# Layer-norm transposes moved from TensorE to DMA in a two-layer attention and SwiGLU kernel

## The chip, the cores and the metric

One core of a Trainium2 chip. The metric is device time in microseconds (us) of one execution; lower is better. Medians of four to seven executions are quoted. Engine names in the profile: PE is TensorE (matrix multiply), PEld its weight loads, DVE is VectorE, ACT is ScalarE, POOL is GpSimd, SP is SyncE, which issues DMAs here. A DMA "lands" when its data has arrived; "landing" times count from its issue. "SPq" and "ACTq" are the instruction queues of SP and ACT.

## The reference

Two layers, each an attention block A and a gated feed-forward block B, on 2048 tokens of width 1024, with a layer norm before each block. Both layers use the same weights.

```python
def _layernorm(x, axis=-1, eps=1e-5):
    m = jnp.mean(x, axis=axis, keepdims=True); v = jnp.var(x, axis=axis, keepdims=True)
    return (x - m) / jnp.sqrt(v + eps)
# A: q, k, v = x @ wqkv, 32 heads of 32; each token attends to 8 tokens, 2 apart, looking back; then @ wo
# B: (silu(x @ w1) * (x @ w3)) @ w2, inner width 3584
x = A_x
x = x + _A_ref(_layernorm(x), A_wqkv, A_wo)
x = x + _B_ref(_layernorm(x), B_w1, B_w3, B_w2)
x = x + _A_ref(_layernorm(x), A_wqkv, A_wo)
x = x + _B_ref(_layernorm(x), B_w1, B_w3, B_w2)
```

## The kernel before

The tokens are cut into four chunks of 512. A "Q" stage computes q, k and v of a chunk on PE and stores them to DRAM; a "T" stage loads them and does the windowed attention on DVE, with a projection by wo on PE; a "B" stage is the feed-forward of a chunk. Stages of different chunks are interleaved so that PE has matmuls while DVE does attention. A scheduler orders each engine's instructions when the program is built, from estimated times and priorities; at run time each engine works through its own list in that order.

This kernel's matmuls take both operands with the contraction dimension on the 128 partitions, so every normalized chunk `xn` (tokens on partitions) must be transposed into `xnT` (features on partitions). Before, PE does it into PSUM and ACT copies it out:

```python
def ln_chunk(c, psum):
    with hp():                                   # raises the priority by 3000 instructions
        xnT = xtp.tile([P, KT, CH], BF16, name="xnT")          # 2 buffers
        ...                                      # bn_stats, bn_aggr on DVE, sqrt on ACT
        for j in range(TPC):                     # 4 tiles of 128 tokens
            n = c * TPC + j
            xn = xnp.tile([P, D], BF16, name="xn")             # 2 buffers
            nc.vector.tensor_scalar(xn[:], x_sb[:, n, :], mv[:, j, 0:1], rstd[:, j:j + 1],
                                    op0=ALU.subtract, op1=ALU.mult)
            pT = psum.tile([P, KT, P], BF16, name="pT", tag="mm")
            for kk in range(KT):                 # 8 blocks of 128x128
                nc.tensor.transpose(pT[:, kk, :], xn[:, kk * P:(kk + 1) * P], ident[:])
            nc.scalar.copy(xnT[:, :, j * P:(j + 1) * P], pT[:])
    return xnT
```

The first chunk has its own function, which the change leaves on PE. The Q stage, cut, with the DMAs:

```python
for which in range(3):                           # q, k, v
    w = wA.tile([P, KT, D], BF16, name="wqkv", tag="wA")       # 2 MB, 2 buffers, loaded for every chunk
    ... nc.sync.dma_start(w[:, k0:k1, :], wqkv_v[...])
    for t0 in range(0, KT, SG):
        sgt = stg.tile([P, SG, CH], BF16, name="sgt")          # 3 buffers
        ... # 16 matmuls into ps, copied to sgt by ACT
        nc.sync.dma_start(qkv_d[l][which][:, t0:t0 + SG, c * CH:(c + 1) * CH], sgt[:])
    if which == 1 and ln_next is not None:
        pending_ln[ln_next] = ln_chunk(ln_next[1], psQ)        # next chunk's norm
```

All DMAs (weights, stores, loads of q, k, v) are issued from SyncE's one in-order queue.

## Time and profile before

| | before |
|---|---|
| median time | 1692.33 us (1691.25 to 1693.8) |
| PE busy | 1661.5 of 1695.0 us |
| PE transposes after the first chunk | 480, 35.0 us busy, 12.7 us idle just before them |
| DVE, ACT busy | 1142.3, 378.7 us |
| DMA queue | 288 MB, 52.7% of 16 engines |

The profile of before is of an execution of 1696.81 us, not one of the four in the table and slower than all of them; its granted clock was 0.995. From its page, the table of engines (busy us, share of the span, number of instructions):

```profile
PE 1661.5 (98%) x7952; PEld 823.1 (49%) x7952; DVE 1142.3 (67%) x1930; ACT 378.7 (22%) x561; POOL 1.9 (0%) x12
q1 hardware_dynamic: 282800, 288.25, 52.7%
```

PE is the bound: 98% busy. The second line is the DMA queue: packets, MB, and the time of its packets as a share of 16 engines' span.

Groups of instructions by line and shape, before: count, then busy us and mean ns of one, then the idle time of the engine just before them with what ended it.

```profile
L132 PE MATMUL pT<-ident,xn 128*128 128x128 bf16 x480 | 35.0, 224 | 12.7 <-DVE xn L128 9.6 <-DVE x_sb L313 1.4 <-ACT sgt L199 0.6
L133 ACT COPY xnT<-pT 128x1024 bf16<-128x1024 bf16 x60 | 57.7, 1024 | 158.1 <-PE pT L132 153.3 <-PE ps L197 4.7
```

This is the work that the change takes off PE and ACT. The 12.7 us are PE standing still in front of a transpose, mostly for DVE's xn.

### The profile page before, as it was taken

To read this page: it belongs to the slowest core of one execution; us is meant where nothing else is said; L and a number is where in the kernel's file an instruction comes from. 1 tells how busy PE (TensorE), PEld (TensorE's weight loads), DVE (VectorE), ACT (ScalarE), POOL (GpSimd) and SP (SyncE) were. 2 spreads that over 40 slices of the span, in tenths; PEclk is the share of its full clock that TensorE was granted. 3 is DMA by queue.
4 is the path that set the end of the run, shared out by engine and by line. 5 is a ranking of instruction groups with operands and counts; after the bars stand their busy time and mean duration, and the time that the engine had idled before them with its cause. 6 is when DMAs were issued, how large, how long until landed. Compare 5 with 4: busy or idle time off the path is not lost.

```text
span 1695.0 us, 19762 instructions
## 1 busy us (share of the span) xinstructions
PE 1661.5 (98%) x7952; PEld 823.1 (49%) x7952; DVE 1142.3 (67%) x1930; ACT 378.7 (22%) x561; POOL 1.9 (0%) x12
## 2 busy tenths in 40 slices
PE   8999999999999999999999999999999999999999
PEld 5655644444444444554445544455444554444444
DVE  5699999999996821229982399813997159952112
ACT  3433422212213101132022321223212221121100
POOL 0000000000000000000000000000000000000000
PEclk9999999999999999999999999999999999999999
DMA  9976655554454244475434754356542654435443
GB/s 315 325 242 201 223 167 160 174 164 149 142 170 148 95 160 146 149 241 182 128 122 155 244 179 148 97 195 229 185 145 95 200 161 151 149 108 191 149 149 99
DMA packets 282891, 289.51 MB, mean 171 GB/s; under 512 B 6192, under 2 KB 256048, under 8 KB 282672
## 3 DMA queue, kind: packets, MB, share of 16 engines
q1 hardware_dynamic: 282800, 288.25, 52.7%
q8 instruction: 62, 1.02, 0.2%
q14 instruction: 29, 0.24, 0.0%
HBM read 258.87 MB, written 29.36 MB: 170 GB/s over the span
## 4 chain that ended last, share of the span: by engine, by line
PE 51%; DVE 39%; DMA 4%; issue 4%; ACT 2%; DVEq 0%; SPq 0%; ACTq 0%
PE acc L308 15%; PE pu L290 11%; PE pg L286 11%; PE ps L197 10%; DVE tm L261 6%; DVE pr L220 5%; DVE hT L295 4%; PE po L268 3%; DVE pr L170 3%; DVE tm L170 3%; DVE st L119 2%; DVE pr L171 2%; DVE tm L171 2%; DMA qkv_d_1_170<-sgt 2%; DVE x_sb L313 1%
## 5 line engine op out<-in xcount | busy, mean ns | idle before, releaser
L290 PE MATMUL pu<-xnT,w3t 128*128 128x512 bf16 x1792 | 430.9, 380 | 0.0
L286 PE MATMUL pg<-xnT,w1t 128*128 128x512 bf16 x1792 | 430.8, 380 | 0.1
L308 PE MATMUL acc<-w2t,hT 128*128 128x512 bf16 x1792 | 392.7, 379 | 0.8 <-DVE hT L295 0.8
L197 PE MATMUL ps<-xnT,wqkv 128*128 128x512 bf16 x1536 | 340.8, 382 | 4.8 <-ACT sgt L199 3.2
L294 ACT ACTIVATE sg<-pg 128x512 bf16<-128x512 f32 x224 | 133.7, 597 | 679.5 <-PE pg L286 662.9
L197 PEld LDWEIGHTS <-wqkv 128*128 128x128 bf16 x1536 | 220.2, 144 | 118.3 <-issue 10.3
L286 PEld LDWEIGHTS <-w1t 128*128 128x128 bf16 x1792 | 175.5, 98 | 209.0 <-issue 2.2
L290 PEld LDWEIGHTS <-w3t 128*128 128x128 bf16 x1792 | 175.5, 98 | 208.4 <-issue 1.6
L308 PEld LDWEIGHTS <-hT 128*128 128x128 bf16 x1792 | 174.9, 98 | 209.5 <-DVE hT L295 1.5
L220 DVE TENSOR_TENSOR pr<-qT,kT 128x2048 bf16<-128x2048 bf16 x128 | 153.6, 1213 | 170.1 <-DMA kT<-qkv_d_1_170 158.2
L295 DVE TENSOR_TENSOR hT<-sg,pu 128x512 bf16<-128x512 bf16 x224 | 152.0, 679 | 170.8 <-PE pu L290 162.7
L313 DVE TENSOR_TENSOR x_sb<-x_sb,acc 128x512 bf16<-128x512 bf16 x128 | 87.0, 681 | 147.6 <-PE acc L308 147.6
L199 ACT CAST sgt<-ps 128x512 bf16<-128x512 f32 x192 | 112.0, 586 | 229.4 <-PE ps L197 200.9
L261 DVE TENSOR_TENSOR tm<-At,vT 128x2048 bf16<-128x2048 bf16 x128 | 152.8, 1215 | 0.1
L268 PE MATMUL po<-wo,oT 128*128 128x512 bf16 x512 | 127.6, 381 | 7.8 <-DVE oT L172 6.5
L133 ACT COPY xnT<-pT 128x1024 bf16<-128x1024 bf16 x60 | 57.7, 1024 | 158.1 <-PE pT L132 153.3
L268 PEld LDWEIGHTS <-oT 128*128 128x128 bf16 x512 | 48.9, 97 | 89.8 <-DVE oT L172 39.5
L170 DVE TENSOR_TENSOR pr<-pr 128x1024 bf16<-128x1024 bf16 x128 | 86.0, 678 | 0.0
L170 DVE TENSOR_TENSOR tm<-tm 128x1024 bf16<-128x1024 bf16 x128 | 84.6, 682 | 0.0
L119 DVE BATCH_NORM_STATS2 st<-x_sb 128x6 f32<-128x512 bf16 x120 | 75.7, 672 | 6.8 <-DMA x_sb<-in_A_x_dram 6.5
L272 DVE TENSOR_TENSOR x_sb<-x_sb,po 128x1024 bf16<-128x1024 bf16 x32 | 38.7, 1210 | 25.1 <-PE po L268 25.1
L171 DVE TENSOR_TENSOR pr<-pr 128x512 bf16<-128x512 bf16 x128 | 52.2, 414 | 0.1
(203 smaller groups left out, 514.5 us busy)
## 6 DMA issues: line engine op xcount, KB each, us to landing
w1t<-in_B_w_dram SPq DMA_DIRECT2D x56, 1024.0 KB, 5.3
w3t<-in_B_w_dram SPq DMA_DIRECT2D x56, 1024.0 KB, 7.2
w2t<-in_B_w_dram SPq DMA_DIRECT2D x48, 1024.0 KB, 5.4
wqkv<-in_A_wqkv_dram SPq DMA_DIRECT2D x23, 2048.0 KB, 8.1
w2t<-in_B_w_dram SPq DMA_DIRECT2D x16, 512.0 KB, 5.1
qkv_d_0_166<-sgt SPq DMA_DIRECT2D x16, 256.0 KB, 4.8
qkv_d_1_167<-sgt SPq DMA_DIRECT2D x16, 256.0 KB, 5.0
qT<-qkv_d_0_166 SPq DMA_DIRECT2D x8, 512.0 KB, 4.8
```

The costliest lines, as they stand in the source:

```text
L170: nc.vector.tensor_tensor(buf[:, 0:4, :], buf[:, 0:4, :], buf[:, 4:8, :], op=ALU.add)
L171: nc.vector.tensor_tensor(buf[:, 0:2, :], buf[:, 0:2, :], buf[:, 2:4, :], op=ALU.add)
L197: nc.tensor.matmul(ps[:], lhsT=w[:, kk, t::KT], rhs=xnT[:, kk, :], start=(kk == 0), stop=(kk == KT - 1))
L199: nc.scalar.copy(sgt[:, t - t0, :], ps[:])
L220: nc.vector.tensor_tensor(pr[:], qT[:], kT[:, :, k0:k0 + TCH], op=ALU.mult)
L261: nc.vector.tensor_tensor(tm[:], At[:], win, op=ALU.mult)
L268: nc.tensor.matmul(ps[:, hh, :], lhsT=oT[:, t, j * P:(j + 1) * P], rhs=wo[:, t, hh * 512:(hh + 1) * 512], start=(t == 0), stop=(t == KT - 1))
L286: nc.tensor.matmul(pg[:], lhsT=w1t[:, kk, fi * P:(fi + 1) * P], rhs=xnT[:, kk, :], start=(kk == 0), stop=(kk == KT - 1))
L290: nc.tensor.matmul(pu[:], lhsT=w3t[:, kk, fi * P:(fi + 1) * P], rhs=xnT[:, kk, :], start=(kk == 0), stop=(kk == KT - 1))
L294: nc.scalar.activation(sg[:], pg[:], ACTF.Silu)
L295: nc.vector.tensor_tensor(hT[:, g0 + fi - f0, :], sg[:], pu[:], op=ALU.mult)
L308: nc.tensor.matmul(acc[:], lhsT=hT[:, f - f0, j * P:(j + 1) * P], rhs=w2ts[(f - f0) // 8][:, (f - f0) % 8, :], start=(f == f0), stop=(f == ...
```

## The change

Intent: PE is the bound, so take the transposes off it, and let the DMA hardware transpose from SBUF to SBUF. The norm of the next chunk is also emitted earlier, to give the slower path more lead. A tile that only warmed PE up was dropped, and some small buffers were cut, to make room for a third xn.

```diff
-    xnp = ctx.enter_context(tc.tile_pool(name="xn", bufs=2))
+    xnp = ctx.enter_context(tc.tile_pool(name="xn", bufs=3))
...  (the warm-up matmuls read a part of hT in place of a tile of their own; mv1, sd1: 4 -> 2 buffers)
-    def ln_chunk(c, psum):
+    def ln_chunk(c):
...
-                pT = psum.tile([P, KT, P], BF16, name="pT", tag="mm")
-                for kk in range(KT):
-                    nc.tensor.transpose(pT[:, kk, :], xn[:, kk * P:(kk + 1) * P], ident[:])
-                nc.scalar.copy(xnT[:, :, j * P:(j + 1) * P], pT[:])
+                nc.sync.dma_start_transpose(out=xnT[:, :, j * P:(j + 1) * P], in_=xn[:])
...
-            if which == 1 and ln_next is not None:
-                pending_ln[ln_next] = ln_chunk(ln_next[1], psQ)
+            if which == 0 and ln_next is not None:
+                pending_ln[ln_next] = ln_chunk(ln_next[1])
```

More of the change, by code (lines that the diff above doesn't have):

```diff
@@ L96 @@
         nc.sync.dma_start(x_sb[:, j:j + 1, :], xin[:, j:j + 1, :])
-    warm = const.tile([P, CH], BF16, name="warm")
-    nc.vector.memset(warm[:], 0.0)
-    preload = small.tile([P, 1], FP32, name="preload")
+    hT = const.tile([P, HTN, CH], BF16, name="hT")
+    nc.vector.memset(hT[:, 0, :], 0.0)
+    preload = small.tile([P, 1], FP32, name="preload", bufs=1)
     nc.scalar.activation(preload[:], epst[:], ACTF.Sqrt)
@@ L102 @@
         pw = psB.tile([P, CH], FP32, name="pw", tag="mm")
-        nc.tensor.matmul(pw[:], lhsT=warm[:, 0:P], rhs=warm[:], start=True, stop=True)
-    hT = const.tile([P, HTN, CH], BF16, name="hT")
+        nc.tensor.matmul(pw[:], lhsT=hT[:, 0, 0:P], rhs=hT[:, 0, :], start=True, stop=True)
     wo = const.tile([P, KT, D], BF16, name="wo")
@@ L141, in stats @@
             st = small.tile([P, 2, 6], FP32, name="st1")
-            mv = small.tile([P, 2], FP32, name="mv1", bufs=4)
+            mv = small.tile([P, 2], FP32, name="mv1", bufs=2)
             for hh in range(2):
@@ L145, in stats @@
             nc.vector.bn_aggr(mv[:], st[:])
-            sd = small.tile([P, 1], FP32, name="sd1", bufs=4)
+            sd = small.tile([P, 1], FP32, name="sd1", bufs=2)
             nc.scalar.activation(sd[:], mv[:, 1:2], ACTF.Sqrt, bias=epst[:])
@@ L178, in q_stage @@
         if xnT is None:
-            xnT = ln_first() if (l, c) == (0, 0) else ln_chunk(c, psQ)
+            xnT = ln_first() if (l, c) == (0, 0) else ln_chunk(c)
         for which in range(3):
@@ L274, in b_stage @@
     def b_stage(c, last):
-        xnT = ln_chunk(c, psB)
+        xnT = ln_chunk(c)
         for (f0, f1) in fsplits:
```

## The prediction

> **What bounds the kernel now.** TensorE. The page's first table has PE busy 1661.5 of 1695.0 us (98%); DVE 1142.3 (67%), ACT 378.7 (22%), DMA 52.7% in the queue table. The chain of waits is 51% PE. The 7424 large matmuls issue every 216 ns in long runs (128 acc matmuls in 27.63 us), an estimate of 1603 us together. So about 90 us of the span is not large matmuls, and only that can be won. In stretches of 50 us DVE is also full from 100 to 500 us (48 to 50 us), and DMA only from 0 to 100 us (0.91 and 0.99).
>
> **What is removed.** 480 PE transposes with their 60 PSUM copies. Groups by line: 35.0 us PE busy, 12.7 us PE idle just before them (9.6 of it waiting for xn on DVE), 57.7 us ACT (60 x 1024 ns). In the timeline a group of eight displaces about 0.45 to 0.6 us of PE or more. Together about 48 us of PE time, almost all on PE's path, since PE is hardly idle elsewhere (33.5 us in total). The norm of a gate/up stage now takes its PSUM slots from the pool of the accumulators, in program order, so its transposes sit at the stage's boundary (540 to 547 us). Without PSUM they can run a stage ahead.
>
> **What is added.** 60 DMA transposes of 256 KB, SBUF to SBUF, 15.7 MB beside 289.5 MB: bandwidth is no problem on average. The Trainium skill, "DMA: Bandwidth & Descriptors", section "Latency and other measured facts", gives 261 GB/s for one kernel's transposes; an estimate from that is 1.0 us each, 60 us of full DMA. No run here shows it yet. I expect 3 to 8 us to landing, since ordinary 256 KB stores here land in 3.2 to 5.0 us. SyncE's queue is in order, and it waits long for buffers to come free (386 us before w2 loads for PE): a transpose can sit behind a waiting load, and a later load behind a transpose that waits for xn. A fourth xn (three buffers) then blocks DVE. Where the norm is computed a stage ahead this is hidden. It is not hidden between 0 and 150 us, where DMA is full, stores of q, k, v are already on the chain (10.9 us at 61 us), and the norm must be ready in a few tens of us; hence the earlier emission between q and k. I charge 5 to 12 us for this.
>
> **Sum.** 1693 - 48 + about 12 = 1657 us. Range 1640 to 1695. Chances: faster by over 2% 0.54, within 2% 0.34, slower 0.12.
>
> **What would show it.** PE busy near 1625 us; no pT group on PE or ACT; ACT near 320 us; PE idle before wqkv and pg matmuls not above a few us per stage, released by the transposes' landing if at all; transposes landing in 3 to 8 us; the start of the first pg right behind the last acc. Matmul spacing stays 216 ns and the granted clock 0.99 or more.
>
> **What would make it wrong.** Transposes of 10 us or more, or slow to issue on SyncE: then weight loads come late, with PE idle before pg, pu and acc, and the time could pass 1700. DVE (full from 100 to 500 us) could swallow the gain there as longer waits for oT. Stores and q/k/v loads held up behind transposes would lengthen the attention stages' wait for kT (158 us now). If none of these bite, the full 48 us give 1645.

## More of the kernel before

Who PE waited for in all of before (us in total, times, longest):

```profile
PE pT L132 <- DVE xn L128: 9.6, 9, 2.7
PE po L268 <- DVE oT L172: 6.5, 13, 2.2
PE ps L197 <- ACT sgt L199: 3.2, 3, 2.0
```

Three stretches of before: PE, PEld, DVE, ACT, POOL busy (instructions), granted clock, DMA share, GB/s. DMA is busiest while the four chunks' q, k, v are computed:

```profile
0.00:160.00 160.00, 146.95 (x727) 92.08 (x728) 124.26 (x228) 60.57 (x96) 1.89 (x12) 0.97 0.83 278
160.00:700.00 540.00, 535.05 (x2557) 252.88 (x2556) 427.54 (x723) 110.97 (x159) 0.00 (x0) 1.00 0.49 156
700.00:1700.00 1000.00, 979.46 (x4672) 478.10 (x4669) 590.49 (x980) 207.11 (x306) 0.00 (x0) 1.00 0.50 161
```

The chain that ended last has two lines that serve as milestones: the first long q/k/v run of layer 1, and the last run of feed-forward accumulations (start, duration):

```profile
708.68 13.83 PE ps L197 x64
...
1670.51 20.73 PE acc L308 x96
```

## The result, and the profile after

The change takes the median from 1692.33 to 1670.78 us (1669.33 to 1672.0). The ratio is 0.9872, with a 95% interval of 0.9855 to 0.9889: 1.3% faster.

The engines and the DMA queue, after:

```profile
PE 1628.0 (98%) x7472; PEld 794.8 (48%) x7472; DVE 1143.0 (69%) x1930; ACT 329.3 (20%) x507; POOL 1.9 (0%) x12
q1 hardware_dynamic: 346160, 303.99, 59.4%
```

The profiled execution is the fastest of the four (1669.33 us, clock 0.997), so the two profiles lie 27 us apart, 6 us more than the medians. PE lost 33.5 us of busy time and ACT 49.4. The span fell by 27.7 us only (1695.0 to 1667.3), so PE's idle time grew from 33.5 to 39.3 us. Where it now stands still (waits of PE, after):

```profile
PE po L264 <- DVE oT L168: 13.6, 15, 2.4
PE ps L193 <- DMA wqkv<-in_A_wqkv_dram: 4.9, 1, 4.9
PE ps L193 <- ACT sgt L195: 4.2, 6, 2.0
PE pT L153 <- DVE xn L150: 3.5, 4, 1.2
```

The 9.6 us in front of transposes are gone, but the waits for DVE's oT have doubled, a wait of 4.9 us for weights appears in a Q stage, and the one for ACT's copies (which wait for stores to free sgt) goes from 3.2 to 4.2 us. The same three stretches, after:

```profile
0.00:160.00 160.00, 143.03 (x645) 88.10 (x646) 125.14 (x229) 49.35 (x85) 1.89 (x12) 0.97 0.96 300
160.00:700.00 540.00, 532.06 (x2448) 246.98 (x2447) 431.06 (x730) 97.92 (x144) 0.00 (x0) 1.00 0.56 167
700.00:1700.00 1000.00, 952.92 (x4383) 459.70 (x4381) 586.78 (x973) 182.06 (x278) 0.00 (x0) 1.00 0.54 167
```

In the first 160 us DMA went from 0.83 to 0.96 busy. The milestones, after:

```profile
699.73 13.83 PE ps L193 x64
...
1643.25 20.73 PE acc L304 x96
```

The kernel is 9.0 us ahead at the first milestone and 27.3 us at the second. Layer 1 alone gained 18.3 us with the transposes of 8 chunks between the milestones, 0.57 us for each group of eight transposes, which is about a group's busy time before (35.0 us / 60 = 0.58). Other runs repeat it: from the first q/k/v matmul of layer 1 to the last accumulation, before took 982.7 us and e8 and e10, which are before in layer 1, 981.5 and 981.1; the change took 964.4, and e3, e9 and e11, which are the change there, 964.0, 965.2 and 963.7. The 7 chunks before the first milestone should have given 16 us at that rate, and gave 9.

Where PE stands still for DVE is much the same in layer 1 with and without the transposes. From 700 us on, the waits for xn and oT together were 9.7 us in before (5.0 and 4.7), and the waits for oT alone were 8.9 us after, 8.7 in e2 and 11.0 in e1 (both below).

What the added DMA looks like, in the answer about the tile xnT, after (duration of the issue in ns, min/median/max, then first and last start in us; the second line is the time from issue to landing):

```profile
L129 SPq DMA_TRANSPOSE xnT<-xn x60: 1231/1302/3577, 23.5 to 1484.5; - x60
...
DMA to landing us min/median/max: 3.1/3.4/8.4
```

PE never waited for a transpose's landing. The last chunk's was issued by 1484.5 us, and its B stage starts at about 1519 (the accumulations before it run from 1498.21 us, for 20.72): there the transposes do run well ahead, as hoped, where before they stood at the stage's boundary.

### The profile page after: what moved, and what is told of

Read it like the earlier page. It is cut to its first block, busy times and chain, and to the rows that moved or that the text cites. A ratio compares the mean times of both kernels' runs of the same rounds, so it can differ in the third digit from the quotient of the medians.

```text
span 1667.3 us, 18841 instructions
## 1 busy us (share of the span) xinstructions
PE 1628.0 (98%) x7472; PEld 794.8 (48%) x7472; DVE 1143.0 (69%) x1930; ACT 329.3 (20%) x507; POOL 1.9 (0%) x12
## 2 busy tenths in 40 slices
DMA packets 346247, 305.18 MB, mean 183 GB/s; under 512 B 69552, under 2 KB 319408, under 8 KB 346032
## 3 DMA queue, kind: packets, MB, share of 16 engines
q1 hardware_dynamic: 346160, 303.99, 59.4%
## 4 chain that ended last, share of the span: by engine, by line
PE 51%; DVE 40%; DMA 4%; issue 4%; ACT 1%; SPq 0%; DVEq 0%; ACTq 0%
PE acc L304 15%; PE pg L282 12%; PE pu L286 12%; PE ps L193 9%; DVE tm L257 6%; DVE pr L216 6%; DVE hT L291 4%; PE po L264 4%; DVE tm L166 4%; DVE pr L166 3%; DVE st L118 2%; DVE tm L167 2%; DVE pr L167 2%; DVE x_sb L309 1%; DVE At L251 1%
## 5 line engine op out<-in xcount | busy, mean ns | idle before, releaser
L264 PE MATMUL po<-wo,oT 128*128 128x512 bf16 x512 | 127.4, 380 | 16.9 <-DVE oT L168 13.6
L167 DVE TENSOR_TENSOR tm<-tm 128x512 bf16<-128x512 bf16 x128 | 51.3, 421 | 0.1
```

What stands on the lines that cost most here:

```text
L167: nc.vector.tensor_tensor(buf[:, 0:2, :], buf[:, 0:2, :], buf[:, 2:4, :], op=ALU.add)
L264: nc.tensor.matmul(ps[:, hh, :], lhsT=oT[:, t, j * P:(j + 1) * P], rhs=wo[:, t, hh * 512:(hh + 1) * 512], start=(t == 0), stop=(t == KT - 1))
```

## The experiments

Two shortfalls needed a cause: the removal was to give 48 us of PE time, and the addition was to cost some 12. Theories, as named in the expectations: **A**, the DMA engines are full at the start and the transposes push weights and stores back; **B**, DVE is full from 100 to 550 us and PE's saved time comes back as waits for DVE; **C**, transposes hold SyncE's in-order queue, and the loads and stores behind them come late. The gain is the median of before minus the median of the run, both from the same rounds.

| run | edit | time, us | gain, us |
|---|---|---|---|
| the change | | 1670.78 | 21.6 |
| e1 | no transposes at all | 1662.57 | 32.0 |
| e2 | PE transposes, rest of the change | 1692.77 | 0.6 |
| e3 | the change, norm emitted between k and v | 1668.29 | 25.1 |
| e4 | layer 0's q/k/v chunks on PE | 1673.45 | 21.1 |
| e5 | every DMA transpose twice | 1725.07 | -31.7 |
| e7 | plain DMA copies in their place | 1679.22 | 14.2 |
| e8, e9 | before, after with less DVE work | 1694.19, 1669.35 | 0.4, 25.2 |
| e10, e11 | before, after with less early DMA | 1692.52, 1665.62 | 1.0, 27.9 |
| e12 | two loads held back | 1675.40 | 18.1 |
| e13 | q/k/v stores from ACT's queue | 1684.84 | 8.0 |

### e1: what the removal is worth when the addition costs nothing

```diff
-                nc.vector.tensor_scalar(xn[:], x_sb[:, n, :], ...)
-                nc.sync.dma_start_transpose(out=xnT[:, :, j * P:(j + 1) * P], in_=xn[:])
+                nc.vector.tensor_scalar(xnT[:, :, j * P:(j + 1) * P], x_sb[:, n, :] (viewed as 128 x 8 x 128), ...)
```

> Wrong result on purpose: DVE writes the normalized rows straight into xnT, so nothing is transposed on any engine (after's order of emission kept). This is the change with its added cost set to zero. After ran at 1670.8 us, 20 us short of the 48 us that the transposes had cost. Theory A (the DMA engines are full for the first 150 us, and the transposes of the first chunks push weight loads and stores back) and theory C (a transpose holds SyncE's in-order queue 1.3 us, and the loads behind it come late) both expect 1655 to 1661 us, with the gain made before 150 us and PE idle before ps down from 10.3 to under 5 us. Theory B (DVE is full from 100 to 550 us, so PE time saved there comes back as waits for oT and hT) expects 1666 to 1671 us, with PE still idle 12 us or more before po.

Measured: 1662.57 us (wrong result, as meant), a gain of 32.0. So the removal is worth 32 us, not 48, and the DMA transposes cost the other 6 to 10 (8.2 by the two medians, 10.4 by the two gains; 5.7 and 6.9 against e3, which will turn out to be the same program as the change). Both A and C and B miss a part: the time is just above A's and C's range, below B's; PE's idle time before ps was 8.3 us, where A and C expected under 5; and the waits for oT that B named are still there. PE and its longest waits in e1:

```profile
PE 1626.8 (98%) x7472; PEld 795.0 (48%) x7472; DVE 1140.8 (69%) x1930; ACT 324.8 (20%) x503; POOL 1.9 (0%) x12
```

```profile
PE po L264 <- DVE oT L168: 15.1, 15, 3.1
PE ps L193 <- ACT sgt L195: 4.6, 4, 2.4
...
PE ps L193 <- DMA wqkv<-in_A_wqkv_dram: 2.6, 1, 2.6
```

The span of e1 was 1661.1 us, so PE was idle 34.3 us: no less than before (33.5). Even with free transposes, the idle time in front of them was not won. PE meets DVE later, at the next instruction that needs it.

```profile
688.59 13.83 PE ps L193 x64
...
1636.89 20.73 PE acc L304 x96
```

Against the change, e1 is 11.1 us ahead at the first milestone and 6.4 at the second. What the DMA transposes cost, they cost early: by 200 us e1 had issued 872 matmuls and the change's run 830, an estimate of 9 us at the 0.216 us of a long run's matmul (64 in 13.83; some records can be missing). Some of this may be start-up luck: from 10 to 20 us the granted clock was 1.00 in e1 and 0.66 in the change's run, and at 20 us e1 was 13 matmuls ahead. But e3, with 0.83 there, was 6 ahead of the change at 20 us and 4 behind at 200, so such a lead need not last. Of the 5 us that e1 loses again later, the clock explains some 3 (an estimate): it was 0.97 from 950 to 1000 and from 1150 to 1200 us in e1, and 1.00 there in the change's run.

### e2: everything but the DMA transposes

```diff
-                nc.sync.dma_start_transpose(out=xnT[:, :, j * P:(j + 1) * P], in_=xn[:])
+                pT = psum.tile(...); 8 x nc.tensor.transpose(...); nc.scalar.copy(xnT[...], pT[:])
```

> Only the emission between q and k and the buffer counts of after; all transposes on PE and ACT as before. If the DMA transposes carry the gain, as theories A and C both say, this is within 5 us of before (1688 to 1698 us). If the earlier emission carries a part, it is below 1685.

Measured: 1692.77 us against 1693.39, nothing: within the range for a gain that the DMA transposes carry. The waits are the point:

```profile
PE po L267 <- DVE oT L171: 11.6, 11, 2.1
...
PE pT L131 <- ACT xnT L132: 2.7, 7, 0.6
...
PE pT L131 <- DVE xn L127: 0.5, 1, 0.5
```

With a third xn and another emission place, the wait in front of the transposes for xn fell from 9.6 to 0.5 us, with the transposes still on PE. The wait for oT rose from 6.5 to 11.6 us, PE's idle time stayed (33.5 and 32.7 us), and so did the median time. So the 12.7 us idle before the transposes were not a separate cost that can be added to their busy time. (The profiled execution was the fastest of e2's four, at 1688.18 us, with a granted clock of 1.000 where the profile of before had 0.995; the 8 us between these two lie in PE's busy time.)

### e3: only the DMA transposes, emission as before

```diff
-            if which == 0 and ln_next is not None:
+            if which == 1 and ln_next is not None:
```

> After, with the next chunk's norm emitted between k and v again. If the placement matters, because DMA transposes need the longer lead, this loses 3 to 10 us against after (1674 to 1681) in the first 150 us, with PE waiting for the transposes' landing before ps. If the scheduler's priority boost places the norm anyway, it stays within 3 us of after's 1671.

Measured: 1668.29 us, 25.1 less than before. A comparison of the built programs shows the same instructions in the same order as the change on PE, DVE, ACT and SP. With DMA transposes the scheduler places the norm alike, wherever it is emitted, as the second case of the expectation has it; this half of the change does nothing. (With PE transposes it does change the order: e2 was built both ways, and the two programs differ.) It is also a repeat of the change: 21.6 and 25.1 us show how far two measurements of one program lie apart, and differences of 3 us below are to be read with that.

### e4: the first layer's q/k/v chunks back on PE

```diff
-                nc.sync.dma_start_transpose(...)                       # all chunks
+                if psum is None: nc.sync.dma_start_transpose(...)      # as before when called for q/k/v chunks 1 to 3
+                else: (8 PE transposes and the copy by ACT)
```

> After, but the norms of q/k/v chunks 1 to 3 of layer 0 are transposed by PE and ACT as before; everything else stays on DMA. In cumulated matmuls after stood 1.8 us behind before at matmul 512 (about 136 us). Theories A and C expect 2 to 6 us gained (1665 to 1669 us), made in the first 150 us, as the DMA engines there are relieved of 12 transposes while PE pays 12 groups of about 0.5 us. Theory B alone expects no gain or a loss of up to 6 us (1670 to 1677).

Measured: 1673.45 us, a gain of 21.1 on before: no better than the change, within B's stated range, outside A's and C's. Within the scatter, 12 DMA transposes cost as much in this stretch as 12 groups on PE do, so placing them by hand on PE wins nothing.

### e8 and e9: room on DVE

```diff
-        for w_ in range(W):
+        for w_ in range(4 if l == 0 else W):      # the other four score products are copied
```

> Wrong result on purpose: before, with half of the DVE score products of layer 0 dropped (4 of 8 shifts, the other 4 copied), some 10 us of DVE work less in each of 8 attention stages between 60 and 550 us. It is the reference for the next run. All theories: between 1670 and 1692 us; DVE no longer full between 100 and 500 us (under 45 of 50 us).

> Wrong result on purpose: after, with the same DVE work dropped. Theory B expects the change to be worth more once DVE has room: 28 to 40 us less than the relieved before, where after is 21.5 us less than before. Theories A and C expect 18 to 24 us, since DMA is as full at the start as it was.

Measured: 1694.19 and 1669.35 us (wrong results, as meant), a difference of 24.8 us, between what the unrelieved program showed twice (21.6 and 25.1). Some 66 us of DVE work (DVE busy 1142.3 to 1076.0 us in before) moved neither kernel. Theory B falls for the stretch that it named: DVE being full in layer 0 is not what eats the gain. All theories missed e8's range, by 2 us. In e9 PE's waits for wqkv were 11.8 us where the change has 4.9: with DVE relieved, PE waited for weights. The test reaches layer 0 only; 8.9 of the change's 13.6 us of waits for oT lie after 700 us, where no DVE work was taken away.

### e5 and e7: more of the transpose, and a plain copy in its place

```diff
+                nc.sync.dma_start_transpose(out=xnT[:, :, j * P:(j + 1) * P], in_=xn[:])   # e5: a second time
...
-                nc.sync.dma_start_transpose(out=xnT[:, :, j * P:(j + 1) * P], in_=xn[:])
+                nc.sync.dma_start(xnT[:, :, j * P:(j + 1) * P], xn[:] (viewed as 128 x 8 x 128))   # e7
```

> After, with every DMA transpose issued twice into the same place (120 in place of 60), same result. Removing them altogether gained 8 us. If their cost is only the full DMA of the first 150 us (theory A) or SyncE's time there (theory C), doubling costs 6 to 14 us, made before 200 us (1677 to 1685 us), and nothing after 700 us, where the norm is a stage ahead. If they cost something in every stage, it is over 15 us, and grows by more than 1 us a stage after 700 us.

> Wrong result on purpose: a plain DMA copy of the same 256 KB from xn to xnT in the transpose's place, the same waits and the same bytes. If bytes on the DMA engines are the cost (theory A as bandwidth) it stays at 1668 to 1672 us. If [...]SyncE's 1.3 us per issue is the cost (theory C), it falls to 1661 to 1666 us, near the run with no transposes (1662.6).

e5 measured 1725.07 us, some 55 us over the change, far above the 6 to 14 that A and C expected. It fits the third case in that text, a cost in every stage: of the loss, 39 us were there at the first milestone (738.37 us) and 56 at the second. But the edit does more than double the cost. The second transpose writes where the first does, so SyncE also waits for the first to land before it issues the second (21.6 us in 14 waits). The waits of PE in e5 show whom that hurts:

```profile
PE ps L194 <- DMA wqkv<-in_A_wqkv_dram: 23.7, 2, 18.9
PE acc L305 <- DMA w2t<-in_B_w_dram: 15.4, 6, 3.8
PE ps L194 <- ACT sgt L196: 14.1, 5, 7.0
PE pu L287 <- DMA w3t<-in_B_w_dram: 8.5, 3, 3.4
```

None of these is a wait for xnT. They are loads and stores that share the queue and the DMA engines with it, in all stages now.

e7 measured 1679.22 us (wrong result, as meant), 8 to 11 us slower than the transposing program, where theory C expected it faster and A the same. Over the whole run the copies' issue was shorter (median 628 ns against 1302), their landing a little later (4.0 us against 3.4). But not where it counts. From 50 to 100 us, first the change, then e7:

```profile
L129 SPq DMA_TRANSPOSE xnT<-xn x4: 1243/1316/3199, 58.1 to 65.6; - x4
DMA to landing us min/median/max: 3.1/4.2/5.7
...
L129 SPq DMA_DIRECT2D xnT<-xn x4: 594/1509/3152, 58.1 to 68.1; - x4
DMA to landing us min/median/max: 2.9/7.2/8.3
```

There a copy was issued no faster than a transpose and landed later, so e7 does not test whether SyncE's issue time is the cost. The loss was made early again, in waits for wqkv (10.4 us) and sgt (9.9 us), in a differently ordered queue; once PE waited 3.4 us for a copy's own landing. The run gives a comparison of cost, too: from the shares of the DMA queue, an estimate of the added DMA time (other transfers' slowing included) is (0.594 x 1667.3 - 0.527 x 1695.0) / 60 = 1.6 us of all 16 engines for a transpose, and (0.578 x 1677.7 - 893.3) / 60 = 1.3 us for the plain copy.

### e10 and e11: room on DMA

```diff
+                if l == 0 and c > 0: k1 = KT // 2            # load half of each q/k/v weight tile, use it twice
                 nc.sync.dma_start(w[:, k0:k1, :], wqkv_v[:, k0:k1, which * D:(which + 1) * D])
```

> Wrong result on purpose: before, loading only the first half of each q/k/v weight tile in chunks 1 to 3 of layer 0 (1 MB in place of 2 MB, nine times) and using it twice. 9 MB less DMA between 45 and 200 us, the same work on every engine. The reference for the next run. Theory A: a small gain on before, 0 to 8 us (1685 to 1693), since its DMA was full only to 100 us.

> Wrong result on purpose: after, with the same 9 MB taken away. Theory A (transposes hurt because the DMA engines are full at the start) expects the difference to the relieved before to grow from 22 to 28-34 us, near what no transposes at all gave (32), with PE waiting for wqkv's landing 2 us or less. Theory C (SyncE's in-order queue is held by the transposes themselves) expects the difference to stay at 20 to 24 us.

Measured: 1692.52 and 1665.62 us (wrong results, as meant). With 9 MB less to load, before gained 1.0 us and the change's kernel 5.2 by its first measurement, 2.7 by e3's. The difference between the two is 26.9 us, between the ranges of A (28 to 34) and C (20 to 24). PE's waits for sgt fell from 4.2 to 1.5 us, but the 4.9 us wait for wqkv stayed, at 4.3. So full DMA engines may be a part of the cost; the evidence, 2 to 5 us, is hardly beyond the scatter of 3.

### e12 and e13: two attempts to do better

```diff
 # e12: a one-column copy by GpSimd makes the load of wo wait for the third score product,
 #      and the first four gate/up weight loads for the k stage of chunk 2 to begin
+                nc.gpsimd.tensor_copy(wo[:, 0, 0:1], psm[:, 2, 0:1])
+                nc.sync.dma_start(wo[:], wo_v)
 # e13
-                nc.sync.dma_start(qkv_d[l][which][...], sgt[:])
+                nc.scalar.dma_start(qkv_d[l][which][...], sgt[:])
```

> After, correct, with 6 MB of loads that are not needed yet taken out of the full stretch: wo waits for the first score products (some 70 us in place of 42 us), the first four gate/up weight tiles wait for the q stage of chunk 2 to end (some 110 us in place of 90 us). Theory A expects 2 to 7 us gained (1664 to 1669 us) before 150 us. Theory C expects no gain (1669 to 1673).

(That text names the q stage of chunk 2; the edit waits for the first k tile after it.)

> After, correct, with the 192 KB-pair stores of q, k and v issued from ACT's queue, right after the copies that fill them; transposes and loads stay on SyncE. The same bytes and the same DMA engines. Theory C (loads and transposes stand in one in-order queue with stores that wait for ACT, and the order costs PE time) expects 3 to 8 us gained (1663 to 1668 us), PE idle before ps under 5 us where after has 10.3. Theory A (full DMA engines) expects no gain (1669 to 1673), or a loss if stores now press harder on the DMA.

("192 KB-pair stores" in that text is a slip: there are 96 stores of 256 KB each.)

Both are correct and both are slower than the change: 1675.40 and 1684.84 us. In e12 the queue was held by my own wait. The long waits in it, one of SyncE and one of PE:

```profile
SPq L222 <- POOL wo L221: 12.0, 1, 12.0
```

```profile
PE ps L193 <- ACT sgt L195: 19.1, 4, 14.6
```

SyncE stood 12.0 us for wo's turn, three stores stood behind it, their sgt buffers stayed full, ACT could not copy, and PE stopped for 14.6 us. From 70 to 80 us DMA was only half busy (0.51): not a full DMA but a held queue stopped PE. The stop cost more than its length: the granted clock was 0.50 from 80 to 90 us and 0.76 from 90 to 100.

In e13 the stores no longer space out SyncE's queue. SyncE issued two gate/up weight loads at 53.0 and 56.6 us, not needed until long after, and then four transposes; the next wqkv followed at 74.2 us. PE waited 9.9 us for it:

```profile
56.63 3.56 SPq L278 DMA_DIRECT2D w3t<-in_B_w_dram  x1
...
60.35 10.92 SPq L129 DMA_TRANSPOSE xnT<-xn  x3
...
74.24 0.67 SPq L180 DMA_DIRECT2D wqkv<-in_A_wqkv_dram  x1
...
84.12 11.04 PE L193 MATMUL ps<-xnT,wqkv 128*128 128x512 bf16 x37 [9.93 <-DMA wqkv<-in_A_wqkv_dram]
```

The 37 matmuls after the wait took 0.30 us each in place of 0.216; the granted clock was 0.50 from 80 to 90 us. ACT, which now issues the stores, was not the brake: PE's waits for its copies were 3.1 us, against 4.2 in the change's run. From 50 to 100 us DMA was full in e13 (a share of 1.11; the shares add up packet times and can pass 1). Issuing itself was slow there: the two gate/up loads above held SyncE 3.57 and 3.56 us, where the change's run, at 90.27 and 93.33 us, shows 0.38 and 0.46. So full DMA engines and a held queue, theories A and C, are not separate causes in this stretch, and it matters which transfers stand first in the queue. The Trainium skill, "DMA: Bandwidth & Descriptors", section "Issuing engines are not separate DMA queues", says that DMAs from all engines run on the same 16 DMA engines, and that issuing from several saves only the sequencer's time. This run fits that: the second issuer brought no gain, and the kernel lost 14 us with the changed order. No version of these beat the change.

## Why the prediction was right or wrong

The measured 1670.78 us lies in the range of 1640 to 1695, but 14 us above the 1657 forecast. "Faster by over 2%" was given 0.54, and "within 2%", which came, 0.34.

- **Right: what is taken off and what is added.** PE busy was foretold near 1625 us and was 1628.0; ACT near 320, and was 329.3; landing in 3 to 8 us, and the median was 3.4; the clock stayed at 0.997. PE never waited for a transpose. The Trainium skill's 261 GB/s ("DMA: Bandwidth & Descriptors", "Latency and other measured facts") gave an estimate of 1.0 us of full DMA each; the queue's shares give an estimate of 1.6 us, or 160 GB/s, here.
- **Right in direction: the stretch where it is not hidden.** Of the 16 us due by the first milestone only 9 came, and e1 shows the cost of the addition as 6 to 10 us in all, where "5 to 12" was charged. Named as the places were the full DMA and SyncE's in-order queue. e12 and e13 show that a held or differently ordered queue can stop PE, though by their own edits; e11 only hints at the full DMA. One wait of the change itself can be read from the traces. The load of wqkv for which PE waited 4.9 us landed 9.8 us after its issue, no later than its fellow in before (10.6 us). It was issued late, at 53.09 us where before has 45.19, behind a store and the load of kT in SyncE's queue, and ahead of the transposes next to it (58.06 us). So, as the traces read, its late place in the queue and not a slower landing made this wait; whether the first four transposes (23.5 to 31.7 us) pushed it back is not shown. How all of the 6 to 10 us split is not settled: every experiment that changed one cause also changed the order of the queue.
- **Wrong: the size of the removal, "together about 48 us of PE time, almost all on PE's path".** It added 12.7 us of idle time to 35.0 us of busy time. e1 measures the removal at 32.0 us, with PE idle 34.3 us in place of 33.5. Most of the busy time was won and the idle time was not. PE waited in front of the transposes because DVE was behind. Without them it arrives at the projection by wo and waits there for oT. e2 shows the trade on its own: waits for xn from 9.6 to 0.5 us, for oT from 6.5 to 11.6 us, PE's idle time and the median time unchanged. With 32 in place of 48 and the charged 12, the sum would have been 1673.
- **Wrong by omission: the earlier emission.** It was taken as a part of the remedy ("hence the earlier emission between q and k"). e3 shows that it leaves every engine's instruction order as it is.
- **The risk of DVE "full from 100 to 500 us"** swallowing the gain there did not come true: e9's gain with 66 us less DVE work is within the scatter of the change's own.

## What to carry to other kernels

When work is taken off the bounding engine, count its busy time as the gain and leave out the idle time just before it, until an experiment shows that the wait does not simply move to the next instruction that needs the same producer. Before adding DMAs to one in-order queue, look at the stretch where DMA is already full, and at what stands behind them there; here most of what the added transfers cost PE was lost in the first 200 of 1670 us. Replacing the new operation by nothing at all (with a wrong result) is a cheap way to split a disappointing gain into "the removal was worth less" and "the addition costs".

## What the Trainium skill lacked or had wrong

- "DMA: Bandwidth & Descriptors" gives 261 GB/s as the rate of DMA transposes of one kernel, and 350 to 400 for contiguous ones; "Advanced Engine Details and Errata", section "X-Bar Transpose (TRN2)", says that transposes are as fast as regular DMAs, and two lines on that they reach about 90% of a copy's bandwidth. For 256 KB from SBUF to SBUF the runs show about 1.6 us of all 16 engines (an estimate from the queue's shares, 160 GB/s) against 1.3 us for a plain copy of the same bytes between the same tiles. To landing, the transpose was no slower: a median of 3.4 us against 4.0.
- No page gives what one SBUF-to-SBUF transpose of this size holds SyncE's queue on trn2: 1.30 us median (at least 1.23), against 0.63 us for the plain copy; nor that issuing takes longer where DMA is full (e13's 1 MB loads: 3.57 us against 0.38).
- No page gives the number of packets of a DMA transpose of this size: the DMA queue's packets rose by 63,360 (282,800 to 346,160) for 60 transposes, 1,056 each, and those under 512 B by as many (6,192 to 69,552).
- "VectorE: DVE Perf Modes", section "The three transpose paths", gives 390 ns for a 128x128 transpose on TensorE and 1309 ns by DMA. That section has no figure for a row of transposes: in rows of eight, PE was busy 0.58 us here for all eight (35.0 us / 60), and 0.57 us per row was gained in layer 1; by DMA, eight blocks in one instruction landed in 3.4 us.
